# The last 64 rows of two heads, and of an output projection, as two 64-column tiles of TensorE

## Chip, cores, metric

One core of a Trainium2 chip. The metric is the device time of one execution in microseconds (us), the median of several runs; a change below about 0.2% can't be told from none.

## What is computed

Three blocks in a row on batches of 8 sequences of 576 tokens: attention of 8 heads of width 64 with a block mask, a mixture of 4 attention experts of which each token uses 2, and a gated MLP.

```python
# 1: attention, 8 heads, blocks of 64
scores = q @ k.transpose(0, 1, 3, 2) / np.sqrt(64)
scores = np.where(block_i >= block_j, scores, -1e9)
x = softmax(scores) @ v                       # -> (8, 576, 512)
# 2: four experts e, each a causal head of width 64
a = softmax(causal((x @ wq[e]) @ (x @ wk[e]).T / np.sqrt(64)))
out += gate[:, :, e] * (a @ (x @ wv[e]) @ wo[e])
# 3: gated MLP
u, v = np.split(np.maximum(out @ w_in, 0), 2, axis=-1)
v_s = w_spatial @ layernorm(v) + b_spatial
result = (u * v_s) @ w_out                    # (8, 576, 512), float32
```

## The kernel before

576 rows are four chunks of 128 and one of 64, and the last chunk fills only half of the 128 partitions. float32 operands are split in two fp16 halves, high and low, and a product is three matmuls (`PROD`: high x high, high x low, low x high).

Heads go in pairs: a batch has four pairs of attention heads and two pairs of experts, 48 pair steps in all. For a pair, `scores` (line 348) makes the scores; its two heads use the upper and the lower 64 partitions of the array (row tiles, `64*128` in the profile), except for the last 64 rows of both heads, which are put together as 128 stationary columns and use the whole array (line 384). `weights` and `weights_t` make the fp16 halves of the exponentials and transpose them by DMA into the tile `pT`. `av` (line 440) multiplies them with the values, in three pieces: chunk 3 (24 matmuls), chunks 2 and 0 (24), chunks 1 and 4 (42). In chunk 4 (line 460) each head reads 128 columns of `pT`, though only 64 of the rows that come out are its own; the others hold finite numbers that nobody uses. Each matmul there has 128 stationary columns and streams 64 or 65 columns of values (the 65th is a one, for the sum). VectorE then takes the reciprocals of the sums and multiplies (lines 464 to 471), and `halves` (line 474) splits the result in fp16 halves (ScalarE or VectorE, then VectorE at line 484) and sends it through a DMA transpose.

`vproj` (line 819) projects the values of the experts, and the gate's logits, chunk by chunk: 12 matmuls of 260 columns a chunk (line 826). `outp` (line 987) is the last projection: 12 matmuls of 512 columns a chunk (line 997), in steps of chunks 0 and 1, 2 and 3, and 4. For chunk 4 they have 64 stationary columns (`128*64`). ScalarE evicts to the tile `o`, of which there is one buffer (line 1000), and SyncE stores it (line 1003).

The order of the work is a table of numbers, `ORDER`: every step is cut in pieces, the table says which step's piece comes next, and so fixes the order of the instructions on each engine. `WAYS` says which engine does a piece where there is a choice. SyncE issues loads, DMA transposes and stores in that order, on one queue. PSUM is four buffers (`duo`) of two banks each.

Of the kernel before, what the change touches and what calls it, by code (L numbers as in the profile page):

```python
# [11 lines left out]
BF = mybir.dt.bfloat16  # L12
# [9 lines left out]
P = 128  # L22
# [10 lines left out]
def attn_moe_gmlp_kernel(  # L33
# [16 lines left out]
    nc = tc.nc  # L50
    V, A, G, T = nc.vector, nc.scalar, nc.gpsimd, nc.tensor
# [5 lines left out]
    KD = DM // P  # L57
# [14 lines left out]
    cst = ctx.enter_context(tc.tile_pool(name="cst", bufs=1))  # L72
# [84 lines left out]
    x_t = buffers("x", 8, 2 * 640, F16)  # L157
    buffers("xh", 2, 2 * 640, F16)
    V16 = cst.tile([P, E, NC, 130], F16, name="V16")
    junk = cst.tile([P, 640], BF, name="junk")  # L160
    for n in range(4):
        G.memset(nat_t[:, n, :, 4], 0.0)
# [107 lines left out]
    def mags(b, pr, i, way):  # L270

        s = BS.setdefault(b, Obj())
        if not hasattr(s, "st"):
            s.st = sm.tile([P, 3, NPAIR], F32, name="mst")
        t = PD[b, pr].nat
        a = slice(0, 2) if i == 0 else slice(2, 3)
        if way == "A":
            for z in range(2):
                A.activation(junk, t[:, z].rearrange("p c d -> p (c d)"), AF.Abs, accum_out=s.st[:, z, pr:pr + 1])
            return  # L280
        V.tensor_reduce(s.st[:, a, pr:pr + 1], t[:, a].rearrange("p i c d -> p i (c d)"), op=OP.max, axis=AX.X,  # L281
                        apply_absolute_value=True)
# [157 lines left out]
    def av(p, wt):  # L440

        ps = duo().rearrange("p (h n) -> p h n", h=2)

        def chunk(c, hh, col, nk, pT):
            o = 65 * c
            for kk in range(nk):
                for i, (t, a, n) in enumerate(((0, 0, 65), (0, 66, 64), (1, 0, 65))):
                    T.matmul(ps[:, hh, o:o + n], pT[:, col(t, kk):col(t, kk) + P], p.v[:, hh, kk, a:a + n],  # L448
                             start=kk == 0 and i == 0, stop=kk == nk - 1 and i == 2)
        for hh in range(2):  # L450
            chunk(3, hh, lambda t, kk: P * (8 * t + 4 * hh + kk), 4, p.pT[0])
        yield
        for hh in range(2):
            chunk(2, hh, lambda t, kk: P * (8 * t + 4 * hh + kk), 3, p.pT[1])
            chunk(0, hh, lambda t, kk: P * (8 * t + 4 * hh + 3), 1, p.pT[1])
        yield
        for hh in range(2):
            chunk(1, hh, lambda t, kk: P * (9 * t + 2 * hh + kk), 2, p.pT[2])

            chunk(4, hh, lambda t, kk: P * (9 * t + 4 + kk) + 64 * hh, 5, p.pT[2])  # L460
        yield
        ov = ps[:, :, 0:325].rearrange("p h (c d) -> p h c d", d=65)
        r = sm.tile([P, 2, NC], F32, name="rr")
        V.tensor_scalar(r, ov[:, :, :, 64], 32e-9, None, op0=OP.add)
        yield
        V.reciprocal(r, r)
        yield
        if wt is not None:
            V.tensor_mul(r, r, wt())
            yield  # L470
        V.tensor_mul(ov[:, :, :, 0:64], ov[:, :, :, 0:64], r.unsqueeze(3).to_broadcast([P, 2, NC, D]))
        p.x32 = ov[:, :, :, 0:64]

    def halves(p, way):
# [289 lines left out]
    def dense(b, keep):  # L764
# [54 lines left out]
        def vproj(cs):  # L819
            n = len(cs)  # L820
            ps = duo().rearrange("p (c m) -> p c m", c=2)[:, 0:n]
            for i, c in enumerate(cs):
                m = 0
                for d in range(KD):
                    for l, r in PROD:
                        T.matmul(ps[:, i, :260], x16[d][:, l, P * c:P * c + P], wvg16[:, r, d, :], start=m == 0,  # L826
                                 stop=m == 11)
                        m += 1
            yield
            for i, c in enumerate(cs):  # L830
# [156 lines left out]
        def outp(cs):  # L987
# [1 line left out]
            ps = duo().rearrange("p (c m) -> p c m", c=2)[:, 0:n]  # L989
            o = mine("o").rearrange("p (c m) -> p c m", c=2)[:, 0:n]  # L990
            gT = R["gT"]
            r = P if cs[0] < 4 else 64
            for i, c in enumerate(cs):
                m = 0
                for d in range(KD):
# [577 lines left out]
```

## Time and profile before

| | us |
|---|---|
| median of 3 runs (1094.84 to 1095.64) | 1095.04 |
| the profiled execution | 1096.49 |
| its span on the core | 1094.8 |
| TensorE busy | 892.7 |
| VectorE busy | 832.1 |
| ScalarE busy | 660.9 |
| mean granted clock of TensorE | 0.933 of 2.4 GHz |

The span runs from the first to the last instruction of the program. Busy times overlap, and matmuls are pipelined: a matmul's recorded time is longer than its distance to the next, so distances between starts are read from the time line. The chain of waits is followed back from the last instruction, at each step to what released it or to the instruction before it on its engine.

### The profile page before, as it was taken

The page shows a single profiled execution, that of the slowest core. Times are in us where ns is not written, and L with a number is a line of the kernel's source. Part 1 is how long each engine was busy: PE and PEld are TensorE (multiplying, and loading weights), DVE is VectorE, ACT ScalarE, POOL GpSimd, SP SyncE. Part 2 cuts the span into 40 slices and gives each one's busy share as a digit, 9 for nine tenths or more (in the row PEclk, how much of TensorE's full clock was granted, in tenths as well). Part 3 has the DMA queues.
Part 4 walks back from the last instruction along what each step waited for, and adds up shares of the span by engine and source line. Part 5 has one row for each costly group of instructions (what it writes and reads, how often), then busy time and mean ns, then how long its engine had stood idle before and what let it go on. Part 6 is the DMA issues. An engine that isn't in the chain of part 4 may idle for free.

```text
span 1094.8 us, 25341 instructions
## 1 busy us (share of the span) xinstructions
PE 892.7 (82%) x10170; PEld 646.5 (59%) x10170; DVE 832.1 (76%) x1730; ACT 660.9 (60%) x1140; POOL 383.4 (35%) x309
## 2 busy tenths in 40 slices
PE   0466667758989799699988888997989989898978
PEld 0245555546566466466666556754767577566644
DVE  2689989999877877867777889768797887757541
ACT  2758566675667555666567668665566764536332
POOL 6054413143154221433252425543354342304210
PEclk9968787888889899899999999998999999999989
DMA  9536989699289786669929997789578537933601
GB/s 223 139 70 145 191 163 181 127 163 172 51 145 157 153 174 119 114 119 173 170 36 171 190 168 120 136 153 184 108 131 157 112 51 101 197 53 61 125 5 44
DMA packets 497719, 143.68 MB, mean 131 GB/s; under 512 B 485440, under 2 KB 491728, under 8 KB 497600
## 3 DMA queue, kind: packets, MB, share of 16 engines
q1 hardware_dynamic: 483760, 134.03, 67.3%
q0 software_dynamic: 2176, 5.25, 1.9%
q10 hardware_dynamic: 11664, 2.76, 1.6%
q8 instruction: 80, 1.31, 0.5%
q14 instruction: 39, 0.32, 0.1%
HBM read 38.19 MB, written 9.44 MB: 44 GB/s over the span
## 4 chain that ended last, share of the span: by engine, by line
PE 26%; DVE 14%; DMA 6%; ACT 6%; issue 4%; SPq 3%; POOL 2%; DVEq 0%; ACTq 0%; POOLq 0%
PE duo L977 5%; PE duo L997 5%; PE duo L448 4%; DMA pT<-p 4%; PE duo L803 2%; PE duo L882 2%; PE duo L826 2%; ACT pf L412 2%; DVE st L391 2%; PE duo L369 2%; PE duo L961 2%; SPq L438 2%; DVE vn L926 1%; DVE bs L890 1%; DVE qk L233 1%
## 5 line engine op out<-in xcount | busy, mean ns | idle before, releaser
L431 POOL TENSOR_TENSOR p<-pf,p 128x1024 f16<-128x1024 f32 (+1 forms) x106 | 205.7, 1943 | 330.5 <-ACT p L327 189.1
L412 ACT ACTIVATE pf<-duo,st,es 128x512 f32<-128x512 f32 (+3 forms) x256 | 139.8, 621 | 75.0 <-DVE st L403 58.9
L448 PEld LDWEIGHTS <-pT 128*128 128x128 f16 x4320 | 149.0, 100 | 30.4 <-DMA pT<-p 13.6
L391 DVE TENSOR_REDUCE st<-duo 128x2 f32<-128x1024 f32 (+1 forms) x192 | 150.5, 813 | 12.0 <-PE duo L377 5.9
L369 PE MATMUL duo<-qk 64*128 64x256 f16 (+3 forms) x1152 | 114.8, 313 | 45.3 <-ACT pf L412 13.6
L977 PE MATMUL duo<-wsp,vn 128*128 128x288 f16 x896 | 121.1, 289 | 10.4 <-ACT vn L923 6.3
L448 PE MATMUL duo<-v,pT 128*128 128x65 f16 (+1 forms) x2880 | 106.8, 198 | 14.6 <-DMA pT<-p 8.6
L997 PE MATMUL duo<-wo,gT 128*128 128x512 f16 (+1 forms) x480 | 111.2, 388 | 6.8 <-DVE xh L484 3.9
L977 PEld LDWEIGHTS <-vn 128*128 128x128 f16 x896 | 86.9, 98 | 35.0 <-ACT vn L923 6.9
L803 PE MATMUL duo<-x,wqk 128*128 128x288 f16 x768 | 102.5, 295 | 4.7 <-ACT pf L412 1.7
L369 PEld LDWEIGHTS <-qk 64*128 64x128 f16 x1152 | 49.4, 97 | 79.5 <-issue 56.8
L803 PEld LDWEIGHTS <-wqk 128*128 128x128 f16 x768 | 76.4, 100 | 27.1 <-issue 5.6
L997 PEld LDWEIGHTS <-gT 128*128 128x128 f16 (+1 forms) x480 | 47.5, 102 | 62.1 <-issue 12.8
L412 ACT ACTIVATE pf<-duo,st,mt 128x384 f32<-128x384 f32 (+3 forms) x128 | 69.8, 618 | 21.4 <-DVE st L403 19.9
L281 DVE TENSOR_REDUCE mst<-nat 128x1 f32<-128x640 f32 (+1 forms) x51 | 53.8, 1060 | 32.7 <-DMA nat<-in_v_dram 28.2
L327 ACT CAST p<-pf 128x1024 f16<-128x1024 f32 (+1 forms) x70 | 65.5, 943 | 12.8 <-DMA pT<-p 11.0
L331 POOL TENSOR_SCALAR p<-pf 128x1024 f16<-128x1024 f32 (+1 forms) x34 | 32.8, 965 | 112.7 <-DMA pT<-p 49.2
L826 PE MATMUL duo<-wvg,x 128*128 128x260 f16 x480 | 61.6, 290 | 8.2 <-DVE st L403 5.8
L320 PE MATMUL duo<-ident,nat 128*128 128x128 f32 (+1 forms) x320 | 53.6, 300 | 17.3 <-DVE xh L484 5.5
L233 DVE SCALAR_TENSOR_TENSOR qk<-duo,scb,qk 128x640 f16<-128x640 f32 (+1 forms) x64 | 52.6, 843 | 13.5 <-ACT qk L227 13.4
L227 ACT ACTIVATE qk<-duo,scb 128x640 f16<-128x640 f32 (+1 forms) x64 | 47.9, 768 | 24.6 <-PE duo L320 20.6
L920 POOL TENSOR_SCALAR vf<-vf,nw 128x512 f32<-128x512 f32 (+1 forms) x29 | 23.8, 831 | 110.7 <-DVE nw L911 90.0
(257 smaller groups left out, 1747.7 us busy)
## 6 DMA issues: line engine op xcount, KB each, us to landing
out_dram<-o SPq DMA_DIRECT2D x16, 512.0 KB, 3.3
nat<-in_q_dram SPq DMA_DIRECT2D x56, 128.0 KB, 3.1
nat<-in_k_dram SPq DMA_DIRECT2D x56, 128.0 KB, 3.1
nat<-in_v_dram SPq DMA_DIRECT2D x50, 128.0 KB, 2.9
wf<-in_moe_w_in_dram SPq DMA_DIRECT2D x8, 512.0 KB, 5.0
pT<-p SPq DMA_TRANSPOSE x144, 5.0
wf<-in_moe_w_out_dram SPq DMA_DIRECT2D x4, 512.0 KB, 4.9
pT<-in_moe_w_spatial_dram POOLq DMA_DIRECT2D x1, 1152.0 KB, 7.9
```

The source lines that it names most:

```text
L233: V.scalar_tensor_tensor(lo, src, scl, hi, op0=OP.mult, op1=OP.subtract)
L281: V.tensor_reduce(s.st[:, a, pr:pr + 1], t[:, a].rearrange("p i c d -> p i (c d)"), op=OP.max, axis=AX.X, apply_absolute_value=True)
L327: A.copy(hi, src)
L369: T.matmul(ph[:, hh, o:o + w], p.q[hs, a, ts], p.k[hs, bb, 0:w], start=i == 0, stop=False)
L391: V.reduce_max(st[:, 0, 2 * c:2 * c + 2], ph[:, :, off[c]:off[c] + P * (c + 1)], axis=AX.X)
L412: A.activation(pf[:, n * hh + off[c]:n * hh + off[c] + w], ph[:, hh, off[c]:off[c] + w], AF.Exp, bias=st[:, 1, 2 * c + hh:2 * c + hh + 1], ...
L431: (V if way[1] == "D" else G).tensor_sub(lo, src, hi)
L448: T.matmul(ps[:, hh, o:o + n], pT[:, col(t, kk):col(t, kk) + P], p.v[:, hh, kk, a:a + n], start=kk == 0 and i == 0, stop=kk == nk - 1 and ...
L803: T.matmul(ps[:, MID + a:MID + a + w], wqk16[:, l, c, 2 * n + i, :], x16[c][:, r, a:a + w], start=m == 0, stop=m == 11)
L826: T.matmul(ps[:, i, :260], x16[d][:, l, P * c:P * c + P], wvg16[:, r, d, :], start=m == 0, stop=m == 11)
L977: T.matmul(ps[:, MID + a:MID + a + n], vn[:, l, ds_], wsp16[:, r, c, a:a + n], start=i == 0, stop=False)
L997: T.matmul(ps[0:r, i], gT[:, x, d, P * c:P * c + r], wo16[:, y, d, :], start=m == 0, stop=m == 11)
```

## The change

Three places, with the same table of order and the same engines.

In `av`, chunk 4 of both heads is done together. Each matmul has 64 stationary columns: head 0 writes partitions 0 to 63 of its bank, head 1 partitions 64 to 127 of its own, and the two alternate. The halves that nobody writes are set to zero by two more matmuls with a tile of zeros. Since head 1's rows now stand on partitions 64 to 127, a 64x64 copy on VectorE moves them to partitions 0 to 63 behind the multiplication.

In `vproj`, chunk 4 is done twice, on both halves of the partitions, so that the experts' values and gates stand where head 1 of a pair needs them. In `outp`, chunk 4 is split by its output columns: 256 of them on partitions 0 to 63, 256 on 64 to 127; the eviction takes 128x256 and there are two stores.

```diff
+    zer = cst.tile([P, 65], BF, name="zer")
+    V.memset(zer, 0.0)
...
-            chunk(4, hh, lambda t, kk: P * (9 * t + 4 + kk) + 64 * hh, 5, p.pT[2])
+        for kk in range(5):
+            for i, (t, a, n) in enumerate(((0, 0, 65), (0, 66, 64), (1, 0, 65))):
+                for hh in range(2):
+                    o = P * (9 * t + 4 + kk) + 64 * hh
+                    T.matmul(ps[64 * hh:64 * hh + 64, hh, 260:260 + n], p.pT[2][:, o:o + 64], p.v[:, hh, kk, a:a + n],
+                             start=kk == 0 and i == 0, stop=kk == 4 and i == 2)
+        for hh in range(2):
+            T.matmul(ps[64 - 64 * hh:128 - 64 * hh, hh, 260:325], identb[:, 0:64], zer, start=True, stop=True)
...
         V.tensor_mul(ov[:, :, :, 0:64], ov[:, :, :, 0:64], r.unsqueeze(3).to_broadcast([P, 2, NC, D]))
+        V.tensor_copy(ov[0:64, 1, 4, 0:64], ov[64:128, 1, 4, 0:64])
...
-                        T.matmul(ps[:, i, :260], x16[d][:, l, P * c:P * c + P], wvg16[:, r, d, :], start=m == 0,
-                                 stop=m == 11)
+                        for z in range(1 if c < 4 else 2):
+                            w = P if c < 4 else 64
+                            T.matmul(ps[64 * z:64 * z + w, i, :260], x16[d][:, l, P * c:P * c + w], wvg16[:, r, d, :],
+                                     start=m == 0, stop=m == 11)
...
-            r = P if cs[0] < 4 else 64
+            if cs[0] == 4:
+                for d in range(KD):
+                    for x, y in PROD:
+                        for z in range(2):
+                            T.matmul(ps[64 * z:64 * z + 64, 0, 0:256], gT[:, x, d, 512:576], wo16[:, y, d, 256 * z:256 * z + 256],
+                                     start=d == 0 and (x, y) == (0, 0), stop=d == KD - 1 and (x, y) == (1, 0))
+                yield
+                A.mul(o[:, 0, 0:256], ps[:, 0, 0:256], R["co"])
+                yield
+                for z in range(2):
+                    nc.sync.dma_start(out[b, 512:576, 256 * z:256 * z + 256], o[64 * z:64 * z + 64, 0, 0:256])
+                return
+            r = P
```

A loop over the magnitudes' two tensors in `mags` also takes its range from another expression, with the same values.

TensorE at the end of the last attention step of the program, before (`V16` are the experts' values, `gT` the gated activations, `wo16` the output weights):

```order
L448 LDWEIGHTS pT_141
L448 MATMUL duo_63<-V16_144,pT_141 128x64
L448 LDWEIGHTS pT_141
L448 MATMUL duo_63<-V16_144,pT_141 128x65
L997 LDWEIGHTS gT_13454
L997 MATMUL duo_63<-wo16_165,gT_13454 64x512 [waits DVE_49]
```

And TensorE at the same place after the change:

```order
L466 LDWEIGHTS pT_141
L466 MATMUL duo_63<-V16_144,pT_141 64x65
L469 LDWEIGHTS identb_68
L469 MATMUL duo_63<-zer_145,identb_68 64x65
L469 LDWEIGHTS identb_68
L469 MATMUL duo_63<-zer_145,identb_68 64x65
L1010 LDWEIGHTS gT_13768
L1010 MATMUL duo_63<-wo16_167,gT_13768 64x256 [waits DVE_49]
```

The matmuls of chunk 4 write 64 partitions each, two that write zeros follow them, and the projection behind them streams 256 columns instead of 512.

VectorE behind that step, before (`rr` are the reciprocals, `xh` the halves, `hm` maxima of the next stage):

```order
L464 TENSOR_SCALAR rr<-duo 128x10 [waits PE_49]
L466 RECIPROCAL rr<-rr 128x10 [waits DVE_49]
L469 TENSOR_TENSOR rr<-rr,wt 128x10 [waits DVE_49]
L471 TENSOR_TENSOR duo<-duo,rr 128x2x5x64 [waits DVE_49]
L484 TENSOR_TENSOR xh<-duo,xh 128x2x5x64 [waits Activation_49]
L933 TENSOR_REDUCE hm<-x 128x1 [waits DMAHW4_49]
```

And VectorE there after the change:

```order
L473 TENSOR_SCALAR rr<-duo 128x10 [waits PE_49]
L475 RECIPROCAL rr<-rr 128x10 [waits DVE_49]
L478 TENSOR_TENSOR rr<-rr,wt 128x10 [waits DVE_49]
L480 TENSOR_TENSOR duo<-duo,rr 128x2x5x64 [waits DVE_49]
L481 COPY duo<-duo 64x64 [waits DVE_49]
L494 TENSOR_TENSOR xh<-duo,xh 128x2x5x64 [waits Activation_49]
```

The copy stands between the multiplication and the work on the halves, in all 48 steps, and waits for the multiplication.

SyncE's queue at the end of the program, before:

```order
L1003 DMA out_dram<-o 128x2x512 [waits DMAHW1_49,Activation_49]
L1003 DMA out_dram<-o 64x512 [waits DMAHW2_49,Activation_49]
L1003 DMA out_dram<-o 128x2x512 [waits DMAHW3_49,Activation_49]
L1568 UNCONDITIONAL_BRANCH
```

And SyncE's queue there after the change:

```order
L1029 DMA out_dram<-o 128x2x512 [waits DMAHW0_49,Activation_49]
L1016 DMA out_dram<-o 64x256 [waits DMAHW1_49,Activation_49]
L1016 DMA out_dram<-o 64x256 [waits DMAHW2_49]
L1029 DMA out_dram<-o 128x2x512 [waits DMAHW3_49,Activation_49]
```

One store of chunk 4 has become two, ahead of the last store.

## Rows read from the trace of the kernel before

**Rows 1.** The page: busy us, share of the span, instructions of each engine.

```profile
PE 892.7 (82%) x10170; PEld 646.5 (59%) x10170; DVE 832.1 (76%) x1730; ACT 660.9 (60%) x1140; POOL 383.4 (35%) x309
```

**Rows 2.** The page: shares of the span in the chain that ended last.

```profile
PE 26%; DVE 14%; DMA 6%; ACT 6%; issue 4%; SPq 3%; POOL 2%; DVEq 0%; ACTq 0%; POOLq 0%
```

**Rows 3.** Busy time by stretch: all engines, then line 448 alone (PE, PEld).

```profile
432.00:1094.80 662.80, 584.89 (x6678) 416.10 (x6674) 481.36 (x1023) 392.94 (x669) 235.59 (x178) 0.97 0.67 119
...
0.00:432.00 432.00, 63.83 (x1620) 60.13 (x1620) 0.87 0.79 149
432.00:1094.80 662.80, 93.75 (x2700) 88.88 (x2700) 0.97 0.67 119
```

**Rows 4.** Pieces of the chain in order: start us, us, engine and line.

```profile
452.06 3.21 PE duo L448 x90
...
469.43 1.27 PE duo L448 x42
...
516.87 2.71 PE duo L997 x12
...
771.98 1.34 PE duo L826 x12
...
838.64 5.18 PE duo L997 x24
...
941.33 2.72 PE duo L997 x12
...
1026.10 2.75 PE duo L448 x90
...
1029.53 0.84 DVE duo L471
```

**Rows 5.** Time line of TensorE, three places: first start us, us to the last end.

```profile
600.56 1.44 PE L448 MATMUL duo<-V,pT 128*128 128x65 f16 x42
601.93 2.78 PE L997 MATMUL duo<-wo,gT 128*64 128x512 f16 x12
604.64 0.76 PE L320 MATMUL duo<-ident,nat 128*128 128x128 f32 x5
...
730.22 0.82 PE L369 MATMUL duo<-qk 64*128 64x512 f16 x6
730.88 0.19 PE L379 MATMUL duo<-m_col,m_row 64*128 64x64 bf16 x2
...
1008.24 0.19 PE L373 MATMUL duo<-t_col,t_row 64*128 64x64 bf16 x2
1008.27 0.19 PE L377 MATMUL duo<-t_col,t_row 64*128 64x64 bf16 x2
```

**Rows 6.** Groups by line and shape: count, busy us, mean ns, idle before.

```profile
L997 PEld LDWEIGHTS <-gT 128*64 128x64 f16 x96 | 10.6, 115 | 15.2 <-issue 7.1 <-DVE qk L816 0.2
L448 PEld LDWEIGHTS <-pT 128*128 128x128 f16 x4320 | 149.0, 100 | 30.4 <-DMA pT<-p 13.6 <-issue 10.9
L471 DVE TENSOR_TENSOR duo<-duo,rr 128x640 f32<-128x640 f32 x48 | 39.7, 828 | 0.9
L464 DVE TENSOR_SCALAR rr<-duo 128x10 f32<-128x10 f32 x48 | 7.8, 162 | 21.8 <-PE duo L448 21.5
L831 ACT ACTIVATE V<-duo,cv 128x256 f16<-128x256 f32 x40 | 18.5, 479 | 22.0 <-PE duo L826 20.4 <-DVE bs L890 1.5
L1000 ACT ACTIVATE o<-duo,hs 64x512 f32<-64x512 f32 x8 | 5.5, 686 | 7.8 <-PE duo L997 4.4 <-DMA out_dram<-o 3.4
```

**Rows 7.** Time line of the tail: ScalarE's evictions and SyncE's store.

```profile
1086.21 0.68 ACT L1000 ACTIVATE o<-duo,hs 64x512 f32<-64x512 f32 x1 [3.41 <-DMA out_dram<-o]
1086.91 0.48 SPq L1003 DMA_DIRECT2D out_dram<-o  x1
...
1089.72 1.11 ACT L1000 ACTIVATE o<-duo,hs 128x1024 f32<-128x1024 f32 x1 [2.84 <-PE duo L997]
```

**Rows 8.** Line 1003 alone: from a store's issue to its landing.

```profile
DMA to landing us min/median/max: 2.2/3.2/5.2
```

More of the change, by code (lines that the diff above doesn't have):

```diff
@@ L277, in mags @@
         if way == "A":
-            for z in range(2):
+            for z in range(a.start, a.stop):
                 A.activation(junk, t[:, z].rearrange("p c d -> p (c d)"), AF.Abs, accum_out=s.st[:, z, pr:pr + 1])
```

## The prediction

> **What bounds the kernel now.** I read the page's busy line first: TensorE is busy 82% of the span, VectorE 76% [rows 1]. Neither is full, so the chain of waits comes next: of the span it puts 26% on TensorE and 14% on VectorE, 6% each on DMA and ScalarE, 3% on SyncE's queue [rows 2]. Its shares add up to 61%, because the chain can be followed back only to 432 us; of the 663 us behind that TensorE has 43%, VectorE 23%. It changes engine every few microseconds, so a cut on one engine is worth something only where a piece of the chain lies on it, and only until the next path is late. In the same stretch VectorE is busy 481 of 663 us and ScalarE 393 [rows 3].
>
> The pieces that the change touches lie on that chain often. 48 attention steps end in the matmuls of line 448 (90 each: 18 steps before 432 us, 30 after, by the counts of [rows 3]). Of those 30, 17 have their closing part on the chain, from the piece at 452.06 to the one at 1026.10 [rows 4]. Of the eight output projections of the last 64 rows, four are there as pieces of 12 (516.87, 602.00, 830.26, 941.33 [rows 4]) and one more is in the tail.
>
> **Part by part.** *Attention, last 64 rows.* Before: 30 matmuls with 128 stationary columns that stream 64 or 65. A piece of 42 takes 1.27 us, 0.030 each [rows 4], so 30 take 0.91. After: the same 30 with 64 stationary columns, in 15 pairs for the two halves of the array, and one more pair that writes zeros. What a pair of column tiles costs no row shows. The nearest rows are pairs of row tiles, in the scores: six 512-column matmuls start and are done with in 0.66 us (730.22 to 730.88), three pairs at 0.22, where one 512-column matmul alone takes 5.18 / 24 = 0.216; two 64-column pairs start 0.03 apart (1008.24, 1008.27) [rows 4, 5]. So row tiles run side by side, down to this width. If column tiles do, 16 pairs at 0.03 are 0.48. The other end is no overlap: 32 x 0.030 = 0.97. A weight load of 64 columns is not shorter than one of 128 but longer, 115 against 100 ns [rows 6]; exposed on 32 loads that adds 0.48, so the upper end is 1.45. I take 0.48, the same width on the same array.
>
> The Trainium skill speaks against this choice: TensorEngine Tiling (Array Packing), section Restrictions and Gotchas, says that column tiling excludes the fast weight load, and TensorE: Matmul & The Clock Gate, section LDWEIGHTS, prices an ordinary load at columns / 1.2 ns, an estimate of 53 ns for 64. The trace agrees that the load gets longer, by 15 ns [rows 6]. By the page's figure 32 loads one after another would take 1.7 us and the step would grow by 0.9; two at a time they would take 0.85.
>
> *Switches of tile form.* In the output projection of the last rows, which has 64 stationary columns already, the 42 matmuls from 600.56 should end at 601.83 and the first of the 12 starts at 601.93; those should end at 604.52 and the next line starts at 604.64 [rows 5]. So a switch costs about 0.10 us each way. The attention step gains one on the way in, 48 times, and one on the way out where what follows uses the whole array. By the order of the changed kernel's instructions that is 27 of 48 (19 go on to scores, which switch today as well, two to the narrow output projection): 0.16 us on average. The attention step on TensorE then goes from 0.91 to 0.48 + 0.16 = 0.64: minus 0.27 us, between minus 0.27 and plus 0.70.
>
> *Copy on VectorE.* Both heads now end on different partitions, so a 64x64 copy in PSUM is added behind the multiplication of line 471, and both readers of the tile (ScalarE or VectorE, for the halves) wait for it. No row has it. A line through 128x10 at 162 ns and 128x640 at 828 [rows 6] gives 162 + 54 x 1.06 = 219 ns, and with the usual 0.02 of issue 0.24 us; 48 make 11.5 us of VectorE time. Queued behind it on VectorE are reductions, maxima and splits for the next step. Line 471 is on the chain six times behind 432 us (the last is in [rows 4]): 6 x 0.24 = 1.4. Bounds: these 1.4, and all 11.5.
>
> *Value projection, last rows.* 12 matmuls of 260 columns (1.34 us [rows 4]) become 24 in 12 pairs that write the same rows twice. Side by side they take what they took, plus a switch in and mostly one out: plus 0.2. Three of eight are on the chain (519, 772, 984 us): plus 0.6. Without overlap each costs 1.3 more.
>
> *Output projection, last rows.* 12 matmuls of 512 columns, 12 x 0.216 = 2.59, become 24 of 256 in 12 pairs; 260 columns take 0.112 [rows 4], so 12 x 0.11 = 1.32: minus 1.27. At this width the weight loads are covered by the stream. Switches are as before. Four on the chain: minus 5.1. ScalarE's eviction goes from 64x512 (686 ns) to 128x256 (479 [rows 6]): minus 0.2, off the chain. SyncE issues two stores instead of one, 0.48 more [rows 7]; queued behind it are the transposes of the weights. The stores of the last rows are not on the chain now, so I cost the second one at nothing; if that cover is gone, 8 x 0.5 = 4 us.
>
> *The tail is different.* The output tile has one buffer. Its eviction at 1086.21 waited for a store, not for TensorE; the store behind it goes out at 1086.91 and the quickest landing is 2.2 us, so it lands near 1089.1, and the last eviction starts at 1089.72 when TensorE is done [rows 7, 8]. With TensorE 1.27 earlier, the buffer is late instead: eviction to 1086.7, second store issued near 1087.2, landed near 1089.4, last eviction near 1089.5. The tail gives 0.2 us, not 1.27.
>
> The zero tile, its fill and the edit of the magnitude loop (same range as before) cost nothing that counts.
>
> **The rivals.** *Pairs don't pay at 65 columns.* The two weight loads of a pair go one after the other, each at least as long as the 30 ns that the matmul streams, so that a pair takes some 0.055. For: the longer load of [rows 6]. Against: the row tiles' pairs, whose loads hide [rows 5]. Attention then costs 0.10 more per step instead of 0.27 less; the gain in the output projection stays. 17 steps and their share before 432 us make plus 2.7, and with the terms below the time is near 1097. The Trainium skill has a rule with almost this result (TensorE: Matmul & The Clock Gate, Part 1: starts never closer than about 25 ns); the pairs of [rows 5] speak against it for different tiles, in short bursts only.
>
> *The change doesn't do what it says:* column tiles take turns. The output projection gains nothing, the value projection pays 1.3 + 0.2 eight times, attention 0.97 + 0.16 - 0.91 = plus 0.22 each. On the chain that is 27 x 0.22 + 5 x 1.5 and the copies, some plus 16: 1111.
>
> *VectorE becomes the bound.* Copies stand in front of the chain's next piece more often than the six times counted: VectorE is busy 73% behind 432 us [rows 3], and a PE that is earlier waits for it. If half of the 48 reach the end (plus 5.8) and TensorE's cuts count at a third (minus 4.5) with the 1.0 of the value projection, the time is 1097.3; if three quarters do and cuts count at a fifth, 1102. With cuts at a third it is slower from some 24 copies on that pass through.
>
> **How the numbers follow.** Cuts on the chain behind 432 us: 17 x 0.27 = 4.6, 5.1, and 0.2 in the tail. Ahead of 432 us, by the same shares: 18/30 of 4.6 = 2.8, one output projection at 4/7, 0.7. Together 13.4. Additions: 0.6 and 1.4, and ahead of 432 us 0.4 and 0.9: 3.3. An addition on the chain counts in full. A cut counts until another path is late; with VectorE and ScalarE as busy as they are I let 0.6 of it pass, 8.0 (0.3 and 1 are the ends). The sum is minus 4.7: 1096.5 - 4.7 = 1091.8 for the profiled execution, which was 1.45 us above the median of the timed runs, so 1090.3 for the median.
>
> Chances: this forecast 0.50; pairs that don't pay 0.25; VectorE 0.17; tiles that take turns 0.08. With all cuts passing the time is 1085; the low end of the range is 1084.5, the high end 1101 takes in the second and most of the VectorE case and leaves out the turns. A measurement of this kernel tells about 0.2%, 2.2 us, from no change. Faster by more than that: most of the first case and a little of the others, 0.47; within: 0.22; slower: 0.31.
>
> **What would show it.** In the profile after: starts of the 64-column matmuls in pairs with about 0.03 us between pairs (right), or 0.05 to 0.06 (first rival), or evenly 0.03 apart (turns). The closing part of an attention step, 1.27 us for 42 matmuls now, should be about 1.0 for 44. The 24 of the output projection should take 1.4 us instead of 2.7. The copy should be near 0.22 us, and TensorE's share of the chain should fall while VectorE's rises. In the tail the last eviction should name a store as what it waited for. The forecast is wrong if the copy takes far over 0.3 us, if scores or transposes wait longer for VectorE, or if a weight load shows up between the paired matmuls.

## The result, and the profile after

| | before | after |
|---|---|---|
| median, us | 1095.34 (1094.84 to 1098.34) | 1111.34 (1110.06 to 1112.69) |
| the profiled execution, us | 1096.49 | 1111.33 |
| its span, us | 1094.8 | 1109.6 |
| mean granted clock of TensorE | 0.933 | 0.916 |

The ratio is 1.014, with a 95% interval of 1.0119 to 1.0162: slower by 13 to 18 us. The forecast was 1090.3, the range ended at 1101; both were wrong.

The page of the kernel after, busy us and share of each engine, then the chain's shares:

```profile
PE 887.0 (80%) x10458; PEld 644.5 (58%) x10458; DVE 855.5 (77%) x1779; ACT 658.0 (59%) x1140; POOL 382.5 (34%) x309
...
PE 10%; DVE 5%; ACT 3%; DMA 2%; issue 1%; POOL 1%; SPq 0%; ACTq 0%; DVEq 0%; POOLq 0%
```

TensorE is busy 6 us less than in [rows 1], VectorE 23 us more, of which the copies are 11; a second profile of the unaltered kernel before has 8.5 us more on VectorE by itself (840.6). The chain can be followed back only a short way this time, so the argument that follows goes by waits and by kernels, not by chain shares.

The windows of the kernel after (length, then PE, PEld, DVE, ACT, POOL, the granted clock, DMA share and GB/s):

```profile
0.00:432.00 432.00, 299.42 (x3520) 224.55 (x3520) 354.13 (x720) 264.45 (x467) 147.05 (x131) 0.87 0.78 149
432.00:1109.60 677.60, 587.54 (x6942) 419.90 (x6938) 501.39 (x1061) 393.59 (x673) 235.43 (x178) 0.95 0.65 117
```

Against [rows 3] the second stretch is 677.6 us instead of 662.8, at a granted clock of 0.95 instead of 0.97. The program is already some 4 us late at its start. The multiplication of the 18th attention step, in the kernel before and then in the kernel after:

```profile
429.86 0.83 DVE L471 TENSOR_TENSOR duo<-duo,rr 128x640 f32<-128x640 f32 x1
```

```profile
433.77 0.83 DVE L480 TENSOR_TENSOR duo<-duo,rr 128x640 f32<-128x640 f32 x1
```

So 4 of the 15 us are lost by then and 11 behind it: the loss is spread over the program. (In a second profile of the kernel before this multiplication starts 0.31 us later, at 430.17; at single steps ahead of it the two profiles lie up to 3.2 us apart.)

The time line of TensorE in the kernel after, at two of the changed places (start us, us to the last end):

```profile
555.81 0.35 PE L450 MATMUL duo<-v,pT 128*128 128x65 f16 x6
556.09 0.66 PE L466 MATMUL duo<-v,pT 128*64 128x65 f16 x30
556.58 0.20 PE L469 MATMUL duo<-zer,identb 128*64 128x65 bf16 x2
556.72 0.66 PE L371 MATMUL duo<-qk 64*128 64x384 f16 x6
...
607.10 0.67 PE L466 MATMUL duo<-V,pT 128*64 128x65 f16 x30
607.60 0.20 PE L469 MATMUL duo<-zer,identb 128*64 128x65 bf16 x2
607.63 1.48 PE L1010 MATMUL duo<-wo,gT 128*64 128x256 f16 x24
```

From 556.09 to 556.58 the 30 matmuls of chunk 4 take 0.49 us: 15 pairs at 0.033, the two matmuls of a pair 1 to 5 ns apart. The last pair and the switch to row tiles take 0.14. The switch in: six matmuls at 0.030 from 555.81 end at 555.99, and the tiles start at 556.09, 0.10 later. At 607.63 the projection follows 0.03 behind the zeros, without a switch, and its 24 matmuls take 1.48 us to the last end, where [rows 5] had 2.78.

Groups of the kernel after (count, busy us, mean ns, idle before):

```profile
L466 PEld LDWEIGHTS <-pT 128*64 128x64 f16 x1440 | 27.8, 114 | 2.7
L481 DVE COPY duo<-duo 64x64 f32<-64x64 f32 x48 | 11.2, 233 | 1.7
L490 ACT CAST xh<-duo 128x640 f16<-128x640 f32 x38 | 26.4, 696 | 21.4 <-DVE duo L481 18.8 <-issue 2.4
```

The load of 64 columns takes 114 ns, and the copy 0.233 us. The tail of the kernel after:

```profile
1101.35 0.47 ACT L1013 ACTIVATE o<-duo,hs 128x256 f32<-128x256 f32 x1 [2.92 <-DMA out_dram<-o]
1101.84 1.11 SPq L1016 DMA_DIRECT2D out_dram<-o  x2
1104.52 1.11 ACT L1026 ACTIVATE o<-duo,hs 128x1024 f32<-128x1024 f32 x1 [2.70 <-DMA out_dram<-o]
```

The last eviction now waits for a store. From the eviction of chunk 4 to the last one it is 3.17 us, where [rows 7] had 3.51.

So each local step came out as predicted, and the kernel is 16 us slower. Where do the 16 us come from? The waits of VectorE tell a first part. The kernel before (us in total, times, longest us):

```profile
DVE u L980 <- PE duo L978: 21.6, 10, 4.1
DVE rr L464 <- PE duo L448: 21.5, 15, 7.3
DVE p L431 <- ACT p L327: 18.1, 13, 3.3
```

And the kernel after, the same three waits:

```profile
DVE u L993 <- PE duo L991: 25.8, 15, 4.7
DVE p L433 <- ACT p L329: 21.7, 12, 6.0
DVE rr L473 <- PE duo L469: 16.9, 10, 6.9
```

The wait that the attention tiles can shorten, that of the reciprocals for the last matmul, fell by 4.6 us. It was 21.5 us in 48 steps to begin with. The other two rose by 7.8. Between the two profiles of the unaltered kernel before these three waits differ by 1.5 us at most.

### The profile page after: what moved, and what is told of

It is laid out like the page before. It is cut to its first block, busy times and chain, and to the rows that moved or that the text cites. A ratio compares the mean times of both kernels' runs of the same rounds, so it can differ in the third digit from the quotient of the medians.

```text
span 1109.6 us, 25980 instructions
## 1 busy us (share of the span) xinstructions
PE 887.0 (80%) x10458; PEld 644.5 (58%) x10458; DVE 855.5 (77%) x1779; ACT 658.0 (59%) x1140; POOL 382.5 (34%) x309
## 5 line engine op out<-in xcount | busy, mean ns | idle before, releaser
L371 PE MATMUL duo<-qk 64*128 64x256 f16 (+3 forms) x1152 | 120.1, 322 | 58.0 <-ACT pf L414 21.3
L393 DVE TENSOR_REDUCE st<-duo 128x2 f32<-128x1024 f32 (+1 forms) x192 | 150.5, 813 | 13.9 <-PE duo L379 7.7
L990 PE MATMUL duo<-wsp,vn 128*128 128x288 f16 x896 | 125.0, 294 | 11.6 <-ACT vn L936 6.3
L450 PEld LDWEIGHTS <-pT 128*128 128x128 f16 x2880 | 107.1, 103 | 32.5 <-DMA pT<-p 14.1
L371 PEld LDWEIGHTS <-qk 64*128 64x128 f16 x1152 | 51.7, 99 | 92.7 <-issue 71.1
L450 PE MATMUL duo<-v,pT 128*128 128x65 f16 (+1 forms) x1920 | 78.4, 202 | 15.0 <-DMA pT<-p 7.7
L1023 PE MATMUL duo<-wo,gT 128*128 128x512 f16 x384 | 87.5, 385 | 1.4 <-ACT pf L414 0.8
L414 ACT ACTIVATE pf<-duo,st,mt 128x384 f32<-128x384 f32 (+3 forms) x128 | 69.7, 617 | 23.7 <-DVE st L405 19.2
L322 PE MATMUL duo<-ident,nat 128*128 128x128 f32 (+1 forms) x320 | 57.0, 316 | 20.3 <-DVE xh L494 7.0
L839 PE MATMUL duo<-wvg,x 128*128 128x260 f16 (+1 forms) x576 | 60.5, 283 | 7.9 <-ACT pf L414 5.3
L1023 PEld LDWEIGHTS <-gT 128*128 128x128 f16 x384 | 37.0, 99 | 45.8 <-issue 4.2
```

The source lines that it names most:

```text
L322: T.transpose(ps[:, P * c:P * c + r], p.nat[0:r, i, c, :], ident[0:r, 0:r])
L371: T.matmul(ph[:, hh, o:o + w], p.q[hs, a, ts], p.k[hs, bb, 0:w], start=i == 0, stop=False)
L393: V.reduce_max(st[:, 0, 2 * c:2 * c + 2], ph[:, :, off[c]:off[c] + P * (c + 1)], axis=AX.X)
L414: A.activation(pf[:, n * hh + off[c]:n * hh + off[c] + w], ph[:, hh, off[c]:off[c] + w], AF.Exp, bias=st[:, 1, 2 * c + hh:2 * c + hh + 1], ...
L839: T.matmul(ps[64 * z:64 * z + w, i, :260], x16[d][:, l, P * c:P * c + w], wvg16[:, r, d, :], start=m == 0, stop=m == 11)
L990: T.matmul(ps[:, MID + a:MID + a + n], vn[:, l, ds_], wsp16[:, r, c, a:a + n], start=i == 0, stop=False)
```

## The experiments

Each run has a short name (e1, f4), given with its result. Ratios are to the kernel before, run beside each, with a 95% interval; "us" is the ratio less one, times 1097. "Half" is the time at the lower of TensorE's two clock levels (1.2 GHz), 2 x span x (1 - mean granted clock), as a mean over a kernel's executions; in the kernel before it is 152 us, after the change 188.

### The change in parts

The copy alone, in the kernel before:

```diff
         V.tensor_mul(ov[:, :, :, 0:64], ov[:, :, :, 0:64], ...)
+        V.tensor_copy(ov[64:128, 0, 4, 0:64], ov[0:64, 0, 4, 0:64])
```

> The kernel before with one thing added: a 64x64 copy on VectorE behind each of the 48 multiplications (into rows that nobody uses). If VectorE is the bound (48 copies of 0.23 us reach the end for the most part), this alone is slower by 8 to 12 us with the granted clock as before (0.933). If the loss lies in TensorE's granted clock, the copy's own price is 1 to 3 us, and whatever comes on top goes with a lower clock: about 1 us for each 0.001 of the mean clock.

Measured (e1): 1.0063 (1.0036 to 1.009), plus 6.9 us; half 161. The copy was predicted at 2.3 us, bound 11.5. At 0.233 us each, some 30 of the 48 reach the end instead of 9 or 10 (17 to 42 by the interval).

The attention steps and the value projection as after the change, the output projection as before it:

```diff
-            if cs[0] == 4:
...
-                return
-            r = P
+            r = P if cs[0] < 4 else 64
```

> The changed kernel with the output projection of before: column tiles in attention, the doubled value projection and the copy. By the sum of the prediction the attention cuts 7.4 us on the chain, of which 4.4 pass, and adds 3.3: about 1 us faster than before, 1094. If attention is what lowers the clock, the mean clock is near 0.92 and the time 1105 to 1112; if the loss comes from the projection, 1094 to 1097 at a clock of 0.933.

Measured (e2): 1.0071 (1.0043 to 1.0099), plus 7.8 us; half 171.

The output projection alone, in the kernel before:

```diff
-            r = P if cs[0] < 4 else 64
+            if cs[0] == 4:
...
+                return
+            r = P
```

> The kernel before with the output projection of the last rows in two column tiles and nothing else. By the prediction's sum 6 us of cuts on the chain, 3.6 pass: 1091 to 1093. If TensorE done earlier and idle for longer is what lowers the clock, some of that is lost here too: the clock is below 0.933 and the time 1095 to 1102.

Measured (e3): 1.0017 (0.9989 to 1.0046). TensorE needs 1.27 us less at eight places, and nothing is gained.

The kernel after the change without the copy; head 1's last rows are then read from partitions that hold zeros:

```diff
-        V.tensor_copy(ov[0:64, 1, 4, 0:64], ov[64:128, 1, 4, 0:64])
```

> The changed kernel without the copy on VectorE (the last 64 rows of each pair's second head are left at zero, so the values that follow differ). If the copies are the loss, this is back at 1090 to 1100 with the clock of the changed kernel (0.916). If the clock is the loss, the time stays at 1104 or more as long as the clock stays near 0.916, and falls only as far as the clock rises.

Measured (e4): 1.0105 (1.0064 to 1.0145). Without the copy 11.5 us of the loss are still there.

Both at once, so that only the attention tiles and the value projection are left of the change:

```diff
-        V.tensor_copy(ov[0:64, 1, 4, 0:64], ov[64:128, 1, 4, 0:64])
...
-            if cs[0] == 4:
...
-            r = P
+            r = P if cs[0] < 4 else 64
```

> Column tiles in attention and the doubled value projection alone: neither the copy (the second head's last 64 rows stay zero) nor the new output projection. By the prediction's sum 4 us faster than before. If the copy is most of what attention loses, within 3 us of before; if the clock is, the clock is near 0.925 and the time 5 us or more above before.

Measured (f3): 1.0022 (1.0001 to 1.0043), plus 2.4 us; half 172. These are the parts from which the prediction had minus 3.4: (4.6 + 2.8) x 0.6 of gain and 1.0 for the value projection.

With these the loss can be put together: tiles 2.4, copy 5.4 (from f3 to e2; 3.8 either way), projection 7.6 (from e2 to the changed kernel; 3.9 either way). The sum is 15.4, the changed kernel's loss, and must be, since each step starts where the last one ended. A second way round gives the projection 9.1 (f3 to e4; 5.0 either way) and the copy 3.8 (e4 to after; 5.0 either way, so by itself not clear of noise).

### Does a cut of TensorE's time pass at all?

The kernel before, whole array, with 18 of the 30 matmuls of chunk 4; the other products are left out of the sum:

```diff
-            chunk(4, hh, lambda t, kk: P * (9 * t + 4 + kk) + 64 * hh, 5, p.pT[2])
+            chunk(4, hh, lambda t, kk: P * (9 * t + 4 + kk) + 64 * hh, 3, p.pT[2])
```

> The kernel before with 18 instead of 30 matmuls for the last 64 rows (two of five key blocks are left out, so the last rows' values differ): whole-array matmuls, no tiles, no switches, no copy, 0.36 us less TensorE per step. If less work lowers the clock, the clock falls below 0.928 and the time does not fall, or rises by up to 10 us. If only column tiles do that, the clock stays at 0.933 and the time falls by 3 to 8 us.

Measured (f4): 1.0013 (0.999 to 1.0035); half 167. TensorE has 48 x 12 x 0.030 = 17 us less to do, more than the tiles save, with no tiles, no switch and no copy, and nothing is gained: by the interval 1.1 us at most. The waits of VectorE in this kernel show where it goes:

```profile
DVE u L980 <- PE duo L978: 28.1, 16, 5.0
...
DVE p L431 <- ACT p L327: 19.4, 13, 3.8
DVE xh L484 <- ACT xh L480: 18.7, 15, 2.8
DVE rr L464 <- PE duo L448: 15.5, 13, 5.4
DVE qk L233 <- ACT qk L227: 15.1, 14, 3.0
```

The reciprocals wait 6.0 us less than before. The gating waits 6.5 more for TensorE (21.6), the three waits for ScalarE together 4.8 more (18.1, 16.9 and 13.4 in the kernel before). VectorE meets the next late engine a few microseconds on.

### More work for TensorE

The kernel after, with nine matmuls of the whole array and 65 columns ahead of the tiles (13 us in 48 steps), into columns that nobody reads:

```diff
+        for i in range(9):
+            T.matmul(ps[:, 0, 330:395], p.pT[2][:, P * i:P * i + P], p.v[:, 0, 0, 0:65], start=True, stop=True)
```

> The changed kernel with nine more matmuls in each attention step, ahead of the column tiles: 128 stationary columns, 65 streamed, into PSUM columns that nobody reads. That gives TensorE back the 0.27 us per step that the tiles save, 13 us in all. If the loss is a granted clock that falls because TensorE has less to do, the clock rises from 0.916 to 0.925 or more and the time falls to 1105 or below, though work was added. If the clock has nothing to do with it, the time grows by 2 to 6 us.

Measured (f1): 1.0116 (1.0085 to 1.0147); half 173. That is 2.6 us below the changed kernel, 4.1 either way: the added work costs nothing that can be measured.

The kernel after, each pair of the attention tiles done twice (some 23 us):

```diff
+        for _ in range(2):
...
-                    T.matmul(ps[64 * hh:64 * hh + 64, hh, 260:260 + n], ...)
+                        T.matmul(ps[64 * hh:64 * hh + 64, hh, 260:260 + n], ...)
```

> The changed kernel with the 15 pairs of column tiles in each attention step done twice (the second pass writes the same over the first): 0.45 us more of TensorE per step, in column tiles. If the clock falls because TensorE has less to do, this too raises it to 0.925 or more. If matmuls in column tiles are what the clock counts for less, it stays near 0.916 here, while whole-array matmuls raise it.

Measured (f2): 1.0239 (1.0211 to 1.0267), 10.8 us over the changed kernel; half 183. Half of the added work passes.

The kernel after, and the kernel before, with ten matmuls of 128 columns behind chunk 4 (26 us):

```diff
+        for i in range(10):
+            T.matmul(ps[:, i % 2, 330:458], onesb, identb, start=True, stop=True)
```

> The kernel after the change, with ten extra matmuls in each attention step behind the two that write zeros: whole array, 128 stationary columns that stream 128, into 128 columns of the same PSUM banks that nobody reads. They stand behind the last matmul that VectorE waits for, and cost TensorE some 10 x 0.055 = 0.55 us a step, 26 us in 48 steps. Theory (the loss is TensorE's granted clock, which falls in stretches where TensorE now has less to do): the mean granted clock rises from 0.906 to 0.916 to at least 0.925, the time at half clock falls by 15 us or more, and the time is at or below the changed kernel's ratio of 1.014 (about 1.005 to 1.014), although 26 us of work are added. Rival (the loss comes from the copy, the switches and the stores; TensorE's time is what counts): the added work passes at half or more, and the ratio is 1.025 to 1.035.

> The kernel before the change, with the same ten extra matmuls behind chunk 4 in each attention step; nothing else is changed. Theory (granted clock): the clock rises above 0.933, to 0.94 or more, and pays for part of the 26 us: ratio 0.995 to 1.008. Rival (TensorE's time is what counts): the clock stays at 0.933 and half or more of the 26 us reaches the end: ratio 1.012 to 1.025.

Measured: 1.0221 (1.0202 to 1.024), half 166 (h1, in the kernel after), and 1.012 (1.0099 to 1.014), half 138 (h2, in the kernel before). The clock did what the theory of these runs said: in h2 it rose to 0.942 in the profile, the highest of all. The time did not: 8.9 us over the changed kernel in h1, 13.2 over the kernel before in h2. One premise was false, too: the extra matmuls write the tile that VectorE reads, and VectorE waited for them. The waits of the kernel before with this fill (L462 is the fill):

```profile
DVE rr L466 <- PE duo L462: 36.8, 26, 7.7
```

That is 15.3 us more than the 21.5 of the kernel before, near the 13.2 us by which this kernel is slower. The same fill put together with the attention part and a copy on ScalarE:

> The change in the attention steps and the value projection alone, the output projection of the last rows as before the change, the copy on ScalarE, and the ten extra matmuls behind the zeros. The parts that looked best so far together. Theory (granted clock, and a copy that is cheaper on ScalarE): the clock is 0.93 or more, the ratio 0.995 to 1.004. Rival (added TensorE work counts in full, a copy costs the same anywhere): ratio 1.015 to 1.025.

Measured (h4): 1.0189 (1.0159 to 1.0219), as its rival said. No fill is worth having here.

### The copy on another engine

```diff
-        V.tensor_copy(ov[0:64, 1, 4, 0:64], ov[64:128, 1, 4, 0:64])
+        A.copy(ov[0:64, 1, 4, 0:64], ov[64:128, 1, 4, 0:64])
```

> The kernel after the change, with the copy behind the multiplication on ScalarE instead of VectorE. If the copy costs what VectorE's queue makes it cost (5 to 6 us by the kernel before with the copy alone), the part of the loss that the clock does not explain falls by 3 to 5 us: ratio about 1.010, the granted clock near 0.91 as after the change. Rival (the copy costs by its place in the chain from the multiplication to the halves, on whichever engine): no change or slower, ratio 1.014 to 1.020, since ScalarE's copy waits for VectorE and VectorE's split then waits for ScalarE.

Measured (h3): 1.0166 (1.0141 to 1.019), against 1.014 and 1.0142 with the copy on VectorE. The copy is not measurably cheaper there. That fits a price for its place between the multiplication and the halves, on whichever engine; that ScalarE's queue merely costs as much as VectorE's is not ruled out. In the group of L490 above ScalarE waits 18.8 us for the copy; its counterpart in the kernel before waits 11.1 for the multiplication:

```profile
L480 ACT CAST xh<-duo 128x640 f16<-128x640 f32 x38 | 26.6, 699 | 19.0 <-DVE duo L471 11.1 <-PE duo L379 4.3 <-issue 2.6
```

### What the projection loses by

One store of all 128 partitions instead of two of 64, in the kernel after and with the projection alone:

```diff
-                for z in range(2):
-                    nc.sync.dma_start(out[b, 512:576, 256 * z:256 * z + 256], o[64 * z:64 * z + 64, 0, 0:256])
+                nc.sync.dma_start(out[b, 512:576, :].rearrange("p (z m) -> z p m", z=2), o[:, 0, 0:256])
```

> The changed kernel with one store of 128 rows of 1 KB for the last 64 rows instead of two of 64. The new projection costs 7 us on top of the tiles and only 2 alone. If the second store (eight more issues on SyncE's queue, and the tile o released later) is what it costs, this is 4 to 8 us faster than the changed kernel; if the clock is, it is within 2 us of it with a clock near 0.916.

> The kernel before with only the projection of the last rows in two column tiles, and one store. With two stores it was 0.2% slower than before, where the sum gave 0.3% faster. If the second store ate the gain, this is 2 to 4 us faster than before; if the clock or the next path did, it is within 2 us of before.

Measured: 1.0221 (1.0195 to 1.0247, g3) and 1.0144 (1.0115 to 1.0173, g4): 8.9 and 13.9 us worse than with two stores. The tail of the changed kernel with one store:

```profile
1111.64 0.52 SPq L1015 DMA_DIRECT2D out_dram<-o  x1
1116.49 1.11 ACT L1025 ACTIVATE o<-duo,hs 128x1024 f32<-128x1024 f32 x1 [4.88 <-DMA out_dram<-o]
```

The tile `o` is free 4.85 us after the issue; with two stores it is 2.68 (1101.84 to 1104.52). At the only other eviction that waits for such a store it is 5.09 against 2.90, and in g4 5.16 and 4.89. So this part of the program seems to react to a store that lands late. Two more runs followed, both with the attention part as changed and the old whole-width projection. In the first, the 12 matmuls of chunk 4 stream 256 columns:

```diff
+                        w = 512 if c < 4 else 256
-                        T.matmul(ps[0:r, i], gT[:, x, d, P * c:P * c + r], wo16[:, y, d, :], start=m == 0, stop=m == 11)
+                        T.matmul(ps[0:r, i, 0:w], gT[:, x, d, P * c:P * c + r], wo16[:, y, d, 0:w], start=m == 0, stop=m == 11)
```

> The change in the attention steps and the value projection alone (ratio 1.0071 when it ran), and the 12 matmuls of the output projection's last rows stream 256 columns instead of 512: the other half of these output rows is left out of the sum, the eviction of 64x512 and the one store stay as before the change. TensorE is 1.27 us shorter at eight places, as in the changed kernel, with no second store. If the shorter TensorE piece by itself turns into waits elsewhere: ratio 1.010 to 1.014, as the changed kernel. If the two stores or the eviction are what the changed projection costs: ratio 1.003 to 1.008, no slower than without the cut.

In the second, chunk 4 is stored in two transfers:

```diff
+            if cs[0] == 4:
+                for z in range(2):
+                    nc.sync.dma_start(out[b, 512:576, 256 * z:256 * z + 256], o[0:64, 0, 256 * z:256 * z + 256])
+                return
```

> The change in the attention steps and the value projection alone, the output projection as before, but the last rows are stored by two transfers of 64x256 instead of one of 64x512. If the second store (0.5 us of SyncE's queue ahead of the transposes, and the output tile held until both have landed) is what the changed projection costs: ratio 1.010 to 1.014. If not: 1.005 to 1.009, as without it.

Measured: 1.0044 (1.0025 to 1.0062, i1) and 1.0071 (1.0045 to 1.0098, i2). Neither the shorter piece nor the second store costs anything that can be measured by itself. The changed kernel is 10.5 us above the first of these (3.1 either way), and they differ only in the pairs of column tiles, the eviction of 128x256 and the two stores. Which of them, or which two together, is open.

What can be shown is where a part of the loss stands: VectorE waits longer for ScalarE's halves of the exponentials. These waits with the attention part alone (e2):

```profile
DVE p L433 <- ACT p L329: 15.9, 11, 3.3
```

In the kernel after it is 21.7, longest 6.0 (above), in its second profile 22.0, without the copy (e4) 21.9. In the four kernels with the tiles and the old-width eviction (e2, f3, i1, i2) it is 14.9 to 17.0. At the first place behind the first narrow projection, VectorE in the attention part with two stores (i2), and then in the kernel after:

```profile
399.65 1.23 DVE L433 TENSOR_TENSOR p<-pf,p 128x1024 f16<-128x1024 f32 x1 [2.42 <-ACT p L329]
```

```profile
402.71 1.23 DVE L433 TENSOR_TENSOR p<-pf,p 128x1024 f16<-128x1024 f32 x1 [4.29 <-ACT p L329]
```

The wait is 1.9 us longer. But 2.8 of the 3.1 us between the two starts stood already at the multiplication ahead of the narrow projection (371.45 and 374.27), and can't be its doing. ScalarE's pieces stand behind a transpose there: it lands 6.2 us after its issue in the kernel after, in its second profile and in e4, and 4.4 to 4.5 us after it in e2, f3, i1 and i2.

The longest of these waits, the 6.0, stands farther on. SyncE, ScalarE and VectorE in the kernel after, and the landing of the first of the two transposes:

```profile
748.27 11.34 SPq L440 DMA_TRANSPOSE pT<-p  x2
...
759.99 1.04 ACT L329 CAST p<-pf 128x1024 f16<-128x1024 f32 x1 [4.03 <-DMA pT<-p]
...
761.48 1.22 DVE L433 TENSOR_TENSOR p<-pf,p 128x1024 f16<-128x1024 f32 x1 [5.99 <-ACT p L329]
```

```profile
DMA to landing us min/median/max: 11.7/11.7/11.7
```

The same transpose lands after 11.4 us in the second profile and after 10.9 in e4, but after 6.6 to 7.9 in e2, f3, i1 and i2, 8.1 in the kernel before and 8.5 in e3. Around it VectorE needs 19.2 to 20.0 us from one step's multiplication to the next in the three profiles with both changes and two stores (the kernel after twice, e4), and 14.9 to 16.2 in e2, f3, i1, i2, e3 and the kernel before; the step ahead of it is some 2 us shorter in those three, so some 2 us of the projection's 7.6 stand here. GpSimd's loads for a coming batch go out beside this transpose (747.47 to 752.17 us) and land late as well: the first four after 7.1 to 10.2 us, where i1 has 3.9 to 5.6. So the narrow projection is paid for at least in part in late transposes, which ScalarE and then VectorE wait for. Why they are late with both changes, and not with either alone, was not found.

### The same programs again

Nothing is edited; these show what one kernel does from execution to execution.

> The changed kernel unaltered, beside the next three. The experiments without the new output projection (0.7% slower) and without the copy (1.05%) were compared on their own; if the parts add up, this is 1.2 to 1.5% slower than before with a clock near 0.916.

> The kernel before unaltered, for a second profile: its time is that of before by definition. If the granted clock differs from execution to execution, stretches at half clock start at other places than in the first profile (0.933), and the clock is between 0.92 and 0.935; if it is fixed by the program, it is 0.933 again.

Measured: 1.0142 (1.0104 to 1.018, g1) and 0.9992 (0.997 to 1.0015, g2). The profiled execution of the first has a span of 1122.1 at a clock of 0.906, the kernel before 1094.0 at 0.934.

## The granted clock: a part of the loss, not the whole

The records of the clock show what may be a second part of the loss. Windows of the kernel after, twice a stretch ahead of a fall of the clock and one behind it (the granted clock is the third number from the end):

```profile
558.30:561.30 3.00, 0.87 (x13) 0.61 (x10) 2.90 (x13) 1.50 (x4) 0.00 (x0) 1.00 0.00 0
561.30:564.60 3.30, 3.30 (x16) 2.06 (x14) 3.30 (x5) 1.21 (x2) 0.00 (x0) 0.50 0.00 0
...
599.30:602.30 3.00, 1.06 (x22) 0.89 (x19) 3.00 (x6) 1.21 (x2) 1.72 (x2) 0.99 1.13 216
602.30:605.60 3.30, 3.27 (x54) 3.05 (x55) 2.86 (x12) 3.06 (x6) 0.00 (x0) 0.50 0.98 254
```

The stretches ahead of the falls at the same two places of the program in the kernel before, 4 to 5 us earlier, and its middle from 460 to 740 us, which is never at half clock:

```profile
554.35:557.35 3.00, 1.12 (x15) 0.82 (x12) 2.97 (x9) 1.76 (x4) 0.00 (x0) 1.00 0.01 3
594.56:597.56 3.00, 1.36 (x29) 1.06 (x25) 3.00 (x6) 1.21 (x2) 1.72 (x2) 1.00 1.12 212
...
460.00:740.00 280.00, 253.16 (x3090) 182.07 (x3088) 216.36 (x461) 186.12 (x310) 117.21 (x86) 1.00 0.81 145
```

In the kernel after TensorE waited through 2 of the 3 us and was granted half the clock about when its work came. The time line of TensorE in the kernel after, at the first of the two, and the same wait in the kernel before:

```profile
558.47 0.19 PE L379 MATMUL duo<-t_col,t_row 64*128 64x64 bf16 x2
560.80 3.06 PE L990 MATMUL duo<-wsp,vn 128*128 128x288 f16 x14 [2.13 <-ACT pf L414]
```

```profile
554.52 0.19 PE L377 MATMUL duo<-t_col,t_row 64*128 64x64 bf16 x2
556.60 1.88 PE L977 MATMUL duo<-wsp,vn 128*128 128x288 f16 x14 [1.88 <-ACT pf L412]
```

The scores end at 558.66, and the next matmul waits 2.13 us for ScalarE's line 414. The kernel before waits there too, 1.88 us, and keeps the full clock; at the second place it waits 1.67 us and the kernel after 1.98. So TensorE stood idle 0.25 and 0.31 us longer, about what the tiles save in a step (0.27 predicted). That it waits longer because it is done sooner fits this; that these tenths of a microsecond are what lowered the clock is not shown, nor is it for the other falls. In the same middle the kernel after has a clock of 0.97:

```profile
460.00:740.00 280.00, 248.57 (x3099) 182.03 (x3095) 228.17 (x474) 184.16 (x311) 112.50 (x81) 0.97 0.79 142
```

Priced at half of each microsecond, 40 us more at half clock in the profiled execution are 20 us, and minus 5 would be left, which is the forecast. That price is too high. Over 215 executions of the kernels named here, each set against the mean of its own kernel, a microsecond more at half clock goes with 0.17 us more of span (0.13 to 0.20), presumably since most of those stretches lie beside other work. The six executions with the copy on ScalarE run from 1109.7 us at 0.926 to 1118.4 at 0.906. The run with the shorter projection (i1) bounds it: its mean clock is 0.915, as low as the changed kernel's 0.916, and it is 10.5 us faster, only 4.8 us above the kernel before, the copies included. So the 36 us more at half clock account for some 6 of the 15 us by the executions' price, and i1 speaks for less; the upper bound of a half each would be 18. The price is a correlation: no run changed the clock and nothing else.

## Why the prediction was wrong

*Pairs: right.* 15 pairs in 0.49 us, 0.033 each; predicted were 0.030. The first rival (0.055) and the tiles that take turns are ruled out. The rule of the Trainium skill that was weighed (TensorEngine Tiling (Array Packing), Restrictions and Gotchas: no fast weight load with column tiles) agrees with the trace in that the load takes 114 ns and not 100; beside pairs 0.033 us apart, 30 loads in 0.49 us, it costs nothing that shows.

*Switches: right.* 0.10 us each way.

*The projection's length: right.* The 24 matmuls take 1.48 us to the last end instead of 2.78; predicted were 1.27 us less, measured are 1.30.

*The tail: right in kind.* The last eviction waits for a store, and 0.34 us are gained there, predicted 0.2.

*The copy: mis-sized.* 0.233 us each, as said, but counted as passing only where line 471 stood on the chain, six times behind 432 us. By the three pairs of runs it costs 4 to 7 us instead of the 2.3 in the sum, so 16 to 30 of 48 pass. The chain names one path; that a copy also delays steps that are only just not on it would explain this, and is not shown.

*"A cut counts until another path is late; I let 0.6 of it pass": this is the step that failed.* The overlap was the error: the next path was late at once. A clean cut of 17 us passed at nothing (f4). The tiles without their copy passed at less than nothing, plus 2.4. The number came from no row: it was a guess between 0.3 and 1. Two rows could have bounded it. VectorE waited 21.5 us in all for the attention steps' last matmul (15 of 48 times), and its other waits, for TensorE and ScalarE, were just as large and stood a few microseconds behind. Work added to TensorE at the same place passes at a third to a half (8.9 of 26 us in h1, 10.8 of 23 in f2, 13.2 of 26 in h2), but not always: the 13 us of f1 passed at nothing.

*The output projection: wrong in sign, cause open.* It was to give 5.8 us before the factor; it gives nothing alone and costs 8 on top of the attention part, some of it in transposes that land later. The bound of 4 us for an uncovered second store would not have held it either, and the second store alone costs nothing that can be measured (i2).

*The clock: a missing term.* No sentence of the prediction asked what a TensorE that is done sooner does to its own clock. It is worth at most some 6 us by the executions' price; it is no fourth item of the sum below, but contained in its items.

Put together: forecast minus 4.7, measured plus 15.4, 20.1 apart. Of these 8.0 are cuts that were to pass and didn't, 3.1 the copy (5.4 instead of 2.3), 1.4 the tiles and the value projection (2.4 instead of 1.0), and 7.6 what the narrow projection costs on top.

Of the rivals, *VectorE becomes the bound* came nearest. It said that half of the copies pass while cuts count for little, 1097 to 1102; the attention part alone came out at plus 7.8 us, some 1103. What took the whole kernel past the range is the projection.

No version here beats the kernel before. The nearest that computes the same is the projection alone (1.0017); the tiles without the copy (1.0022) leave out rows.

## What to carry to other kernels

Where several engines take turns on the chain, price a cut by the wait it shortens (its total in the waits of the engine that waits) and by the next wait behind it, not by a factor on the time saved; added work on the same path may still cost up to half of itself, as it did here. A correction step of a fifth of a microsecond that stands in every step between two engines cost more here than the chain's count of it. And look at the granted clock of any kernel in which TensorE is made to finish earlier and wait, but don't price it at its full length.

## What was not expected of the hardware

Column tiles of 64 with 65 streamed columns kept 0.033 us a pair for 15 pairs in a row, though each weight load is recorded at 114 ns. TensorE's granted clock fell to half behind two stretches in which the engine had mostly waited, where the kernel before had waited 0.25 and 0.31 us less and kept the full clock. Its mean was lower in the kernels in which the engine had less to do: 0.931 in the kernel before, as a mean over its executions, 0.924 with 12 matmuls fewer a step (f4), 0.915 with the tiles and a shorter projection (i1); with the copy alone, which takes nothing from TensorE, it was 0.927 (e1). One store from 128 partitions, its two halves side by side in DRAM, held its tile 4.85 us from its issue, two of 64 partitions 2.68 us, for the same bytes.
